# A planned attention + MLP kernel: first loads and clears rearranged, GpSimd casts as plain copies, mixed rows written straight to x, and a rank of its own for every planned operation

## The chip, the cores and the metric

One core of one Trainium2 chip. The metric is device time of one launch in microseconds (us), the median of several runs; less is better. Beside it stands one profiled execution, whose trace is the source of every duration in this text. Engines are PE (TensorE matmul), PEld (TensorE weight load), DVE (VectorE), ACT (ScalarE), POOL (GpSimd) and SP (SyncE, here used only to issue DMAs).

## The reference

Two blocks, one after the other. First a linear attention with exponential features, for batch 8, 8 heads, 576 rows and head size 64:

```python
def phi(x):
    proj = np.einsum('bhsd,df->bhsf', x, w_phi)                      # 64 -> 128 features
    proj = proj - np.max(np.abs(proj), axis=-1, keepdims=True)
    return np.concatenate([np.exp(proj), np.exp(-proj)], axis=-1)    # 256 features
q_p, k_p = phi(q), phi(k)
kv, z = einsum('bhsf,bhsd->bhfd', k_p, v), sum(k_p, axis=2)
attn = einsum('bhsf,bhfd->bhsd', q_p, kv) / (einsum('bhsf,bhf->bhs', q_p, z) + 1e-6)
```

Its heads are laid side by side as x (8, 576, 512). Then a two-layer MLP with layer norm and residual: `xn = (x - mean) / sqrt(var + 1e-6) * g_ln`, `out = x + relu(xn @ w_ch1) @ w_ch2`, with w_ch1 512x2048 and w_ch2 2048x512. Inputs and output are float32; the kernel multiplies in bf16.

## The kernel before

**Tiling.** The batch is cut into four pairs. A pair has 1152 rows, nine tiles of 128: four full tiles of each batch, and a ninth, the *mixed* tile, that holds the last 64 rows of both. Attention runs in 32 *units* of two heads, eight to a pair; units 0 to 3 of a pair belong to its first batch and units 4 to 7 to its second. The MLP of a pair takes its tiles in three groups (4, 3, 2 in the first pair). A group can start when all its rows of x are written, normalized and transposed, so the first group of a pair needs that pair's units 0 to 3, and the mixed tile needs all eight.

**One unit.** q and k are brought to bf16 and transposed: on PE in the first units (L689, mixed rows L697), later by a cast (`cast`, L749-766, on DVE, ACT or POOL) and a DMA transpose on SP (L782). PE makes the projections (L882, L888, L804, L897), DVE takes their absolute maxima (L950, L808), ACT the exponentials (L964, L1058, L967 and the small `em`, `en`), POOL scales v (`vv`, L990-999), PE forms k'v (L1095) and q'kv (L1155, L1163, L1169), and DVE with POOL, or in the first units DVE with ACT, divide and write x. The mixed tile's rows are the special case: the two heads of a unit come out on partition halves 0-63 and 64-127, and one of the two halves lies on the wrong partitions for x. Before, that half goes to a small tile `xs`, and after four units one DMA (`move_rows`, L1120) carries it over; eight such DMAs in all.

**The MLP.** L1420 is the first product (four accumulating matmuls per hidden block), its ReLU runs on ACT or DVE (L1431, L1429), L1489 is the second product, L1454 the last tile's in halves. Results are scaled on ACT or DVE, the residual is added on POOL, and SP stores.

**What sets the order.** The program text does not. Every operation is added to a planner (`Order`) with its possible engines, an assumed duration on each, what it reads and writes, and a rank. `run` plays the program through on these assumed durations: whenever an engine is free, the ready operation of lowest rank goes next, on whichever of its engines is free. The instructions are then emitted in that order, engine by engine, and each engine works its list strictly in order. Where PE has nothing ready in the played-through time and that time is under `WARM = 75.0` us, the planner puts a *filler* on PE's list: a matmul of zeros (L1695). Fillers are ordinary instructions and stay in PE's list whatever the chip does. A rank was before the sum of entries of the table `OFF` (33 stage names, in 13 tables: each of the first eight units has its own, the rest share five) and the operation's latest start worked out backwards:

```python
op.rank = sum(OFF[t][k] for t, k in op.rank) + late
```

DMA issues are planned operations too, each followed by one or more pieces that stand for the transfer. Operations without code (`add("DVE", 3.5, -9.0, None)` and the like, after L1589) stand for the prologue, which is written out by hand at L415-470: loads of w_phi, the identity, clearing of tiles.

Of the kernel before, what the change touches and what calls it, by code (L numbers as in the profile page):

```python
# [11 lines left out]
BF16 = mybir.dt.bfloat16  # L12
# [5 lines left out]
def bcast(ap: bass.AP, dim: int, n: int) -> bass.AP:  # L18
# [20 lines left out]
OFF = (  # L39
    {  # L40
        "load": 291.2, "trans": 545.6, "trans.copy": 61.3, "mixed": 513.4, "mixed.max": -174.1,
        "mixed.exp": 7.7, "mixed.fold": 4.9, "k": 74.4, "k.max": 173.7, "k.em": -451.3,
        "k.exp": 679.6, "en": -537.5, "vv": -95.0, "q": -87.3, "q.max": 488.8, "q.em": 368.3,
        "tails": 57.1, "tails.exp": -236.8, "kv": -216.4, "kv.copy": -163.2, "num0": -302.8,
        "num1": -385.0, "num.dve": 8.3, "g1": 0.0, "g2": 0.0, "g3": 0.0, "put": -147.6,
        "ln": -23.8, "w1": -144.2, "w2": -136.8, "ln.c": -23.8, "ln.t": -23.8,
    },
    {
        "load": 291.2, "trans": 447.4, "trans.copy": 161.0, "mixed": 105.6, "mixed.max": 1.6,
        "mixed.exp": 358.4, "mixed.fold": -27.1, "k": -23.9, "k.max": 92.7, "k.em": -150.0,  # L50
# [12 lines left out]
    },
    {
        "load": 291.2, "trans": 554.4, "trans.copy": 7.7, "mixed": 69.3, "mixed.max": -181.5,
        "mixed.exp": 144.7, "mixed.fold": -51.9, "k": -35.6, "k.max": 154.8, "k.em": 166.9,
        "k.exp": 111.3, "en": -340.2, "vv": -186.8, "q": -229.5, "q.max": 107.7, "q.em": 510.4,
        "tails": 220.4, "tails.exp": -338.9, "kv": -395.7, "kv.copy": 83.0, "num0": -369.5,
        "num1": -379.2, "num.dve": -264.0, "g1": 0.0, "g2": 0.0, "g3": 0.0, "put": 54.2,
        "ln": 107.0, "w1": -144.2, "w2": -136.8, "ln.c": 31.8, "ln.t": 66.5,  # L70
    },
    {
        "load": 272.9, "trans": 530.9, "trans.copy": 207.4, "mixed": 269.7, "mixed.max": -38.1,
        "mixed.exp": 276.4, "mixed.fold": -36.7, "k": 556.5, "k.max": 408.1, "k.em": -190.4,
        "k.exp": 563.2, "en": -354.3, "vv": -281.3, "q": 110.5, "q.max": 541.6, "q.em": 101.1,
        "tails": 326.2, "tails.exp": -391.9, "kv": -247.4, "kv.copy": -205.8, "num0": -198.9,
        "num1": -688.0, "num.dve": -117.6, "g1": -293.1, "g2": -189.2, "g3": -5.0,
        "put": -103.6, "ln": 107.2, "w1": -341.2, "w2": -67.5, "ln.c": 107.2, "ln.t": 107.2,
    },
    {  # L80
        "load": 6.3, "trans": 536.0, "trans.copy": 106.5, "mixed": 212.8, "mixed.max": -321.6,
        "mixed.exp": -375.0, "mixed.fold": 170.2, "k": -2.1, "k.max": 368.9, "k.em": 11.7,
        "k.exp": 156.1, "en": -310.7, "vv": -194.9, "q": 84.5, "q.max": -113.0, "q.em": 400.4,
        "tails": 184.4, "tails.exp": -473.9, "kv": -401.2, "kv.copy": -224.2, "num0": -390.2,
        "num1": -685.7, "num.dve": 7.9, "g1": -233.9, "g2": -41.7, "g3": -19.1, "put": -110.8,
        "ln": -60.0, "w1": -341.2, "w2": -67.5, "ln.c": 107.2, "ln.t": 107.2,
# [273 lines left out]
def kernel(  # L360
# [769 lines left out]
    def a_num(u, part):  # L1130
# [104 lines left out]
        if folded(n):  # L1235
# [19 lines left out]
            if i == 3:  # L1255
                move_rows(u, b, V_put)
# [479 lines left out]
```

## Time and profile before

| | us |
|---|---|
| median of 3 runs (lowest to highest) | 362.01 (361.94 to 362.59) |
| the profiled execution's own time | 362.2 |
| span of its trace | 360.4 |
| PE / DVE / ACT / POOL busy | 354.1 / 250.2 / 264.3 / 208.8 |

The span runs from the first to the last recorded instruction; 1.8 us of the profiled execution lie around it. "Busy" for PE includes the drain of pipelined matmuls and the fillers, so a PE that is busy throughout may still be doing nothing useful. A row of the windows view gives, for a stretch of the span, each engine's busy time with its instruction count in brackets, the granted PE clock as a share of full speed, the mean share of DMA engines busy, and GB/s. A row of the timeline gives start, length, engine, line, operation, output <- input, and in square brackets the engine's idle time before it with what ended it.

### The profile page before, as it was taken

How to read it: one execution, taken by the hardware profiler on the slowest of the kernel's cores; microseconds unless marked ns; L12 is line 12 of the kernel's file. 1: busy time of each engine (PE TensorE's matmuls, PEld its weight loads, DVE VectorE, ACT ScalarE, POOL GpSimd, SP SyncE). 2: the span in 40 equal slices, each digit the busy share in tenths (PEclk: the TensorE clock that was granted, in tenths of full speed). 3: DMA queues.
4: the chain of work that ended last, by engine and by line, in shares of the span. 5: the costliest groups of instructions: out<-in, count | busy, mean ns of one | idle time of the engine just before them, and what ended most of it. 6: DMA issues, size and time to landing. Idle time of an engine off the chain costs nothing.

```text
span 360.4 us, 9697 instructions
## 1 busy us (share of the span) xinstructions
PE 354.1 (98%) x3728; PEld 225.5 (63%) x3728; DVE 250.2 (69%) x575; ACT 264.3 (73%) x580; POOL 208.8 (58%) x363
## 2 busy tenths in 40 slices
PE   7999999999999999999999999999999999999995
PEld 6899966656566655555676555555666665455544
DVE  4788978999889986797779669959896856100001
ACT  1859979689899978796978769858968765364430
POOL 1459795858575658482968478595637484210121
PEclk9999999999999999999999999999999999999999
DMA  7999999999999999998999876976665431600012
GB/s 175 316 232 270 233 235 251 225 269 282 250 184 192 257 232 213 248 185 182 238 292 202 152 194 141 221 190 135 118 88 128 98 88 27 155 31 0 29 60 88
DMA packets 134750, 64.01 MB, mean 178 GB/s; under 512 B 101168, under 2 KB 130224, under 8 KB 134704
## 3 DMA queue, kind: packets, MB, share of 16 engines
q1 hardware_dynamic: 128928, 58.61, 74.2%
q0 software_dynamic: 4256, 4.20, 7.1%
q10 hardware_dynamic: 1520, 0.59, 0.7%
q8 instruction: 29, 0.48, 0.6%
q14 instruction: 17, 0.14, 0.1%
HBM read 36.77 MB, written 9.44 MB: 128 GB/s over the span
## 4 chain that ended last, share of the span: by engine, by line
PE 95%; DMA 2%; DVE 1%; ACTq 0%; ACT 0%; SPq 0%; issue 0%; DVEq 0%
PE b_bank L1420 35%; PE b_bank L1489 34%; PE n_bank L1095 4%; PE a_bank L888 4%; PE n_bank L1695 4%; PE a_bank L1163 2%; DMA qx<-in_k_dram 2%; PE n_bank L1089 1%; PE a_bank L897 1%; PE n_bank L1163 1%; PE a_bank L872 1%; PE b_bank L1454 1%; PE n_bank L1169 1%; PE n_bank L804 1%; PE b_bank L689 1%; PE a_bank L882 1%
## 5 line engine op out<-in xcount | busy, mean ns | idle before, releaser
L1420 PE MATMUL b_bank<-xT,w 128*128 128x384 bf16 (+2 forms) x768 | 146.2, 326 | 0.0
L1489 PE MATMUL b_bank<-w,hT_all 128*128 128x512 bf16 x560 | 142.4, 379 | 0.0
L1420 PEld LDWEIGHTS <-w 128*128 128x128 bf16 x768 | 71.1, 98 | 51.3 <-issue 0.3
L1431 ACT ACTIVATE hT_all<-b_bank 128x384 bf16<-128x384 f32 (+2 forms) x121 | 60.1, 498 | 46.3 <-PE b_bank L1420 45.6
L950 DVE TENSOR_REDUCE m<-a_bank 128x8 f32<-128x1024 f32 x64 | 77.4, 1213 | 18.2 <-PE a_bank L888 13.0
L1489 PEld LDWEIGHTS <-hT_all 128*128 128x128 bf16 x560 | 50.9, 98 | 42.3 <-issue 0.3
L964 ACT ACTIVATE eb<-a_bank 128x1024 bf16<-128x1024 f32 x60 | 61.0, 1040 | 3.8 <-DVE qkT L704 3.0
L1508 POOL TENSOR_TENSOR o<-o,x 128x512 f32<-128x512 f32 x23 | 26.6, 1158 | 49.3 <-ACT o L1502 44.3
L1272 POOL TENSOR_TENSOR x<-numc,rden 128x384 bf16<-128x384 f32 (+1 forms) x56 | 33.9, 612 | 28.3 <-DVE rden L1197 27.5
L990 POOL TENSOR_TENSOR vv<-v,em 128x512 bf16<-128x512 f32 x30 | 31.4, 1047 | 32.6 <-ACT em L955 29.3
L1429 DVE TENSOR_SCALAR hT_all<-b_bank 128x384 bf16<-128x384 f32 (+2 forms) x71 | 39.0, 549 | 7.8 <-PE b_bank L1420 6.5
L967 ACT ACTIVATE qe<-a_bank 128x1024 bf16<-128x1024 f32 x40 | 40.6, 1030 | 3.2 <-PE a_bank L888 1.8
L990 POOL TENSOR_TENSOR vv<-v,en 128x512 bf16<-128x512 f32 x30 | 31.6, 1053 | 0.2
L1341 DVE BATCH_NORM_STATS2 st<-x 128x6 f32<-128x256 bf16 (+1 forms) x68 | 26.5, 427 | 2.4 <-POOL x L1272 2.3
L1497 DVE SCALAR_TENSOR_TENSOR o<-b_bank,rstd,x 128x512 f32<-128x512 f32 x12 | 8.9, 740 | 27.1 <-issue 25.6
L1695 PE MATMUL n_bank<-wz 128*128 128x120 bf16 x381 | 27.6, 223 | 0.0
L1502 ACT ACTIVATE o<-b_bank,rstd 128x512 f32<-128x512 f32 x23 | 15.8, 687 | 14.4 <-PE b_bank L1489 14.2
L1163 PEld LDWEIGHTS <-ea 128*128 128x128 bf16 x448 | 21.5, 97 | 7.2 <-issue 0.2
L1695 PEld LDWEIGHTS <-wz 128*128 128x128 bf16 x403 | 24.4, 102 | 0.8
L1095 PE MATMUL n_bank<-vv,eb 128*128 128x65 bf16 x480 | 24.4, 194 | 0.0
L1095 PEld LDWEIGHTS <-eb 128*128 128x128 bf16 x480 | 20.3, 98 | 4.4
L763 POOL TENSOR_TENSOR b<-qk,one 128x1024 bf16<-128x1024 f32 x11 | 20.8, 1894 | 0.4 <-DMA qkT<-b 0.2
(129 smaller groups left out, 508.8 us busy)
## 6 DMA issues: line engine op xcount, KB each, us to landing
out_dram<-o SPq DMA_DIRECT2D x31, 256.0 KB, 3.1
qk<-in_k_dram SPq DMA_DIRECT2D x12, 512.0 KB, 6.1
qk<-in_q_dram SPq DMA_DIRECT2D x12, 512.0 KB, 7.1
v<-in_v_dram SPq DMA_DIRECT2D x12, 512.0 KB, 5.2
w<-in_moe_w_ch_dram POOLq DMA_DIRECT2D x8, 512.0 KB, 11.5
qk<-in_k_dram SPq DMA_DIRECT2D x8, 256.0 KB, 6.0
v<-in_v_dram SPq DMA_DIRECT2D x8, 256.0 KB, 5.8
qk<-in_q_dram SPq DMA_DIRECT2D x7, 256.0 KB, 6.1
```

The source lines that it names most:

```text
L950: nc.vector.reduce_max(out=m, in_=ps, axis=AX.X, apply_absolute_value=True)
L964: nc.scalar.activation(eb, ps, AF.Exp, scale=(1.0, -1.0)[t])
L967: nc.scalar.activation(qe_bufs[n % 2][:, t].rearrange("p (c h) f -> p h c f", h=2), u["pm", 0].rearrange("p (h c) f -> p h c f", h=2), AF. ...
L990: nc.gpsimd.tensor_tensor(out=u["vv"][:, t, 0:MX, 0:D], in0=vb[:, hh, :].rearrange("p (c d) -> p c d", d=D), in1=bcast(e[:, 0:MX], 2, D), ...
L1095: nc.tensor.matmul(ps[:, t, c // 4, :], EB[:, t, c, :], vv[:, t, c, :], start=False, stop=(t == 0 and c == MX - 1), skip_group_check=True,)
L1163: nc.tensor.matmul(ps[t][:, i, :], ea(u, t, c), KV[:, t, c // 4, :], start=True, stop=True,)
L1272: nc.gpsimd.tensor_tensor(out=x_, in0=num, in1=rd, op=ALU.mult)
L1420: nc.tensor.matmul(st["ps"], w1_sb[:, kc, jj * P : (jj + 1) * P], xT_bufs[(pair * NR + r) % XB][:, kc : m * KC : KC, :], start=(kc == 0), ...
L1429: nc.vector.tensor_relu(h_sb, st["ps"])
L1431: nc.scalar.activation(h_sb, st["ps"], AF.Relu)
L1489: nc.tensor.matmul(ch[t], hT[r, jj][:, rt * P : (rt + 1) * P], w2_sb[:, jj, :], start=(jj == 0), stop=(jj == JC - 1),)
L1695: nc.tensor.matmul(banks[res][i][:, 0:WN] if res else warm, wz, wz[:, 0:WN], start=bool(res), stop=bool(res), skip_group_check=True,)
```

## The change

Four parts.

1. *First loads and clears.* w_phi comes in one DMA of both halves instead of two. The negated identity is made on POOL (a clear and a select) instead of by one DVE multiply; clearing the tails of two `ea` tiles and the second `vx` tile moves from DVE to POOL. The tail loads of v move from ACT's queue to SP's, and the load of ACT's table is added right behind the first main load of q. The assumed prologue durations change accordingly.
2. *POOL casts.* A multiply by a broadcast one becomes `tensor_copy`; the assumed duration of the 1024-column cast goes from 1.87 to 1.02 us, that of the 128-column one from 0.38 to 0.5.
3. *Mixed rows.* Both halves are written straight to x, across partitions where needed; `xs` and the eight DMAs of `move_rows` go.
4. *Ranks.* `OFF` and the backward pass go; a table `RANK` of 2362 integers gives each planned operation its rank by number, in the order in which the operations are added. The numbers came out of a search. The first ones read as follows, with what they belong to: issue of the main loads of unit 0, k 110 (SP) and q 707 (ACT), v 838 (SP); ACT table 753; tail loads of k, halves 0 and 1, 619 and 549 (SP); tail loads of q 1158 and 689 (ACT); tail loads of v 546 and 754 (SP); main loads of unit 1, k 548, q 557, v 825; of unit 2, k 610, q 677, v 1252; of unit 3, k 859, q 779, v 1262 (all SP).

```diff
+RANK = tuple(map(int, """
+515 611 710 638 283 459 110 715 707 715 753 619 716 549 716 1158 717 689 717 838 718 546 719 754
+719 548 720 557 722 379 723 645 825 724 610 729 677 729 1252 729 859 730 779 730 1262 730 852
...
-        latest = {}
-        for op in reversed(self.ops):
...
-                op.rank = sum(OFF[t][k] for t, k in op.rank) + late
+        assert len(self.ops) == len(RANK)
+        for op in self.ops:
+            op.rank = RANK[op.number]
...
-    nc.scalar.dma_start(out=wphi_f[0:D, :], in_=w_phi)
-    nc.scalar.dma_start(out=wphi_f[D : 2 * D, :], in_=w_phi)
+    nc.scalar.dma_start(
+        out=wphi_f,
+        in_=bass.AP(tensor=w_phi.tensor, offset=w_phi.offset, ap=[[0, 2], [F, D], [1, F]]),
+    )
...
+    nident = consts.tile([P, P], BF16, name="nident")
+    nc.gpsimd.memset(nident, 0.0)
+    nc.gpsimd.affine_select(
...
-        nc.vector.memset(eb[:, 2 * MX * P :], 0.0)
+        nc.gpsimd.memset(eb[:, 2 * MX * P :], 0.0)
         ea_bufs.append(eb)
-    clear_vx(vx_bufs[1])
-
-    nident = consts.tile([P, P], BF16, name="nident")
-    nc.vector.tensor_scalar(
-        out=nident, in0=ident, scalar1=minus, scalar2=None, op0=ALU.mult
-    )
+    clear_vx(nc.gpsimd, vx_bufs[1])
...
-                nc.gpsimd.tensor_tensor(
-                    out=out, in0=in_, op=ALU.mult,
-                    in1=bcast(bcast(one[:, 0], 1, in_.shape[1]), 2, in_.shape[2]),
-                )
+                nc.gpsimd.tensor_copy(out=out, in_=in_)
...
-        add(("DVE", "ACT", "POOL"), (Port(0.6), 0.98, 1.87), rank, cast_main, r=[*loaded(u, "q"), *loaded(u, "k")],
+        add(("DVE", "ACT", "POOL"), (Port(0.6), 0.98, 1.02), rank, cast_main, r=[*loaded(u, "q"), *loaded(u, "k")],
...
-            if half == b:
-                dst, w = u["x"][ps_, MX : MX + 1, h * D : (h + 1) * D], [("x", pair, 2, h)]
-            else:
-                i = u["i"] % 4
-                dst, w = xs[ps_, i : i + 1, :], [("xs", b, i)]
-            add("POOL", 0.3, V_put, lambda d=dst, p=ps_: put(d, p, 2, 1), r=rd, w=w)
-        if u["i"] % 4 == 3:
-            move_rows(u, b, V)
+            dst = u["x"][b * 64 : b * 64 + 64, MX : MX + 1, h * D : (h + 1) * D]
+            add("POOL", 0.3, V_put, lambda d=dst, p=ps_: put(d, p, 2, 1), r=rd, w=[("x", pair, 2, h)])
...
-    add("POOL", 1.3, -9.0, None)
+    add("POOL", 4.2, -9.0, None)
     add("SP", 0.72, -9.0, None)
-    add("ACT", 1.85, -9.0, None)
-    add("DVE", 3.5, -9.0, None)
+    add("ACT", 1.3, -9.0, None)
+    add("DVE", 3.88, -9.0, None)
     add("PE", 2.1, -9.0, None)
-    add("DVE", 0.8, -8.9, None, w=["wbk"])
-    add("DVE", 1.1, -8.8, None)
-    add("POOL", 0.7, -8.8, None)
+    add("DVE", 0.47, -8.9, None, w=["wbk"])
     load_main("k", 0, 1, -4.0, "SP")
-    load_tails("k", 0, -3.9, "SP")
     load_main("q", 0, 1, -4.0, "ACT")
-    load_tails("q", 0, -3.9, "ACT")
-    load_main("v", 0, 1, -3.8, "SP")
-    load_tails("v", 0, -3.7, "ACT")
     add(
-        "ACT", 1.3, -1.0,
+        "ACT", 1.3, -3.9,
         lambda: nc.scalar.preload_act_table_set("natural_log_exp_and_others"),
     )
+    load_tails("k", 0, -3.9, "SP")
+    load_tails("q", 0, -3.8, "ACT")
+    load_main("v", 0, 1, -3.7, "SP")
+    load_tails("v", 0, -3.6, "SP")
```

Where a rank was written at the call (`-3.9` and the like), `RANK` now takes its place. The first units' division (`put_row` on DVE or ACT) is changed in the same way as the POOL one shown.

More of the change, by code (lines that the diff above doesn't have):

```diff
@@ L147 @@
+RANK = tuple(map(int, """
[112 rows of a table added]
+""".split()))
 class Op:
@@ L236, in offer @@
             heapq.heappush(events, (op.ready, 1, op.number, op))
-        latest = {}
-        for op in reversed(self.ops):
-            us = [us if isinstance(us, float) else 0.6 for us in op.us]
-            late = min((latest[o.number] for o in op.users), default=1000.0) - op.lag
-            late -= sum(us) / len(us)
-            latest[op.number] = late = late if op.due is None else min(late, op.due)
-            if isinstance(op.rank, tuple):
-                op.rank = sum(OFF[t][k] for t, k in op.rank) + late
+        assert len(self.ops) == len(RANK)
+        for op in self.ops:
+            op.rank = RANK[op.number]
         for op in self.ops:
@@ L423 @@
     make_identity(nc, ident)
+    nident = consts.tile([P, P], BF16, name="nident")
+    nc.gpsimd.memset(nident, 0.0)
+    nc.gpsimd.affine_select(
+        out=nident, in_=nident, compare_op=ALU.not_equal, fill=-1.0, base=0, pattern=[[-1, P]],
+        channel_multiplier=1,
+    )
     wz = consts.tile([P, P], BF16, name="wz")
@@ L467 @@
     w2_loads = {}
-    xs = consts.tile([P, 4, D], BF16, name="xs")
     xc_bufs = [consts.tile([P, n, DM], BF16, name=f"xc{i}") for i, n in enumerate((4, 3))]
@@ L786, in a_trans_dma @@
         rank = rk("trans", n)
-        add(("DVE", "ACT", "POOL"), (0.2, 0.2, 0.38), rank, cast_mixed, r=[*loaded(u, "q"), *loaded(u, "k")],
+        add(("DVE", "ACT", "POOL"), (0.2, 0.2, 0.5), rank, cast_mixed, r=[*loaded(u, "q"), *loaded(u, "k")],
             w=[("b16x", n % NB16)])
-        add(("DVE", "ACT", "POOL"), (Port(0.6), 0.98, 1.87), rank, cast_main, r=[*loaded(u, "q"), *loaded(u, "k")],
+        add(("DVE", "ACT", "POOL"), (Port(0.6), 0.98, 1.02), rank, cast_main, r=[*loaded(u, "q"), *loaded(u, "k")],
             w=[("b16", n % NB16)])
@@ L1113, in a_kv @@
         add(("ACT", "DVE"), (0.28, 0.35), rk("kv.copy", n), copy, r=[("kv", n)], w=[("KV", n % 4)], release=("N", 1), reads="N")
-    def move_rows(u, b, V):
-        half = 1 - b
-        rows = slice(half * 64, half * 64 + 64)
-        def move():
-            nc.sync.dma_start(
-                out=u["x"][b * 64 : b * 64 + 64, MX, :].rearrange(
-                    "p (i two d) -> p i two d", two=2, d=D
-                )[:, :, half, :],
-                in_=xs[rows],
-            )
-        dma("SP", V, 32768, move, row=128, r=[("xs", b, j) for j in range(4)],
-            w=[("x", u["pair"], 2, 2 * j + half) for j in range(4)])
     def a_num(u, part):
@@ L1243, in a_num @@
                 return
[L1244 removed]
+            after = [("x", pair, group_of(pair, t0), h0)]
             for half in range(2):
                 ps_ = slice(half * 64, half * 64 + 64)
[L1247 to L1251 removed]
+                dst = u["x"][b * 64 : b * 64 + 64, MX, (h0 + half) * D : (h0 + half + 1) * D]
                 add(("DVE", "ACT"), (0.19, 0.32), V_put, lambda e, d=dst, p=ps_: put_row(e, d, p),
[L1253 removed]
+                    r=[nk, rn, *after], w=[("x", pair, 2, h0 + half), ("last", n, half)], release=(res, room) if half else None)
                 after = [("last", n, half)]
[L1255 to L1256 removed]
             return
@@ L1557, in moe @@
         return V
-    def stage_table(n):
-        return n if n < H else H + sum(n >= m for m in (H + 4, 2 * H, 2 * H + 4, 3 * H))
     def rk(stage, n):
-        return ((stage_table(n), stage),)
+        return ()
     units, pairs = [], []
```

123 lines of the change are left out of this document (5 added, 118 removed), and 110 rows, old and new, of the table RANK.

## The prediction

> **What bounds the kernel now.** I read the page first (who is busy, when), then the windows view by stage, the fillers alone in that view, PE's waits, and last the timeline of the first 14 us and of the end.
>
> ```profile
> span 360.4 us, 9697 instructions
> ...
> PE 354.1 (98%) x3728; PEld 225.5 (63%) x3728; DVE 250.2 (69%) x575; ACT 264.3 (73%) x580; POOL 208.8 (58%) x363
> ```
>
> PE is the longest engine, but part of that is filler. The filler's line alone (count, shortest/median/longest ns, first and last start), the windows view of that line, and the windows of all engines:
>
> ```profile
> L1695 PEld LDWEIGHTS <-wz x403: 95/98/152, 1.0 to 74.8; 128*128 128x128 bf16 x135
> ```
>
> ```profile
> 0.00:20.00 20.00, 10.64 (x143) 9.59 (x144) 1.00 0.92 255
> 20.00:40.00 20.00, 8.79 (x132) 7.44 (x131) 1.00 1.20 235
> ```
>
> ```profile
> 20.00:75.00 55.00, 55.00 (x844) 41.77 (x842) 49.05 (x114) 46.54 (x100) 41.59 (x75) 1.00 1.16 242
> 75.00:356.00 281.00, 281.00 (x2618) 167.28 (x2617) 188.64 (x424) 208.41 (x466) 159.91 (x272) 1.00 0.76 160
> ```
>
> There are 403 fillers, the last at 74.8 us; 143 lie in the first 20 us and 132 in the next. In the stretch from 20 to 75 us, PE is 55.00 of 55.00 busy only thanks to them. The next three views are PE's waits, the chain that ended last, and PE's groups from 320 to 340 us.
>
> ```profile
> PE n_bank L1692 <- DVE wz L426: 1.0, 1, 1.0
> PE a_bank L882 <- DVE qkT L704: 0.8, 1, 0.8
> PE b_bank L689 <- DMA qk<-in_q_dram: 0.5, 1, 0.5
> PE b_bank L804 <- DVE qkT L704: 0.2, 1, 0.2
> ```
>
> ```profile
> 41.69 1.16 PE b_bank L1695 x22
> ...
> 47.84 1.83 PE b_bank L1420 x8
> ...
> 319.02 7.15 PE b_bank L1420 x44
> ...
> 345.63 7.55 PE b_bank L1489 x35
> 353.19 3.51 PE b_bank L1454 x32
> ```
>
> ```profile
> L1420 PE MATMUL b_bank<-xT,w 128*128 128x384 bf16 x82 | 15.3, 326 | 0.0
> L1489 PE MATMUL b_bank<-w,hT_all 128*128 128x512 bf16 x32 | 8.7, 379 | 0.0
> ```
>
> In the chain a filler costs 1.16/22 = 0.053 us of PE's queue, an L1420 matmul of 384 columns 7.15/44 = 0.163, an L1489 one 7.55/35 = 0.216. Between 320 and 340 us PE therefore did 82 x 0.163 + 32 x 0.216 = 20.3 us of useful work in 20 us: no room there. PE's named waits sum to 2.5 us, all in the first 13 us. So **from 75 us to the last matmul at 353.19 + 3.51 = 356.7 us PE's list runs without a hole, and the time can only be won ahead of 75 us**: the fillers, 403 x 0.053 = 21.4 us, and the 2.5 us of waits. Since PE waits for nobody after 13 us although its list is full of fillers, the list itself sets the pace: the chip is no slower than the planner assumed. A filler less on the list is 0.053 us less, until a real wait appears.
>
> What the fillers stand for is the supply from ACT and DVE. From 20 to 75 us these have 8.5 and 6.0 us idle (55 - 46.54, 55 - 49.05). The start is slow too:
>
> ```profile
> 4.62 0.39 PE L689 MATMUL b_bank<-ident,qk 128*128 128x128 bf16 x4
> ...
> 4.82 0.37 SPq L559 DMA_DIRECT2D qk<-in_q_dram  x1
> 4.83 0.22 DVE L453 CAST wbk<-wphi_f 64x128 bf16<-64x128 f32 x1 [0.46 <-DMA wphi_f<-in_w_phi_dram]
> ...
> 5.21 0.49 DVE L437 MEMSET vx<- 128x520 f32 x1 [0.15 <-issue]
> ...
> 5.96 0.25 DVE L462 TENSOR_SCALAR nident<-ident,minus 128x128 bf16<-128x128 bf16 x1
> 6.13 0.42 DVE L704 COPY qkT<-b_bank 128x512 bf16<-128x512 bf16 x1
> ...
> 6.60 0.61 PE L882 MATMUL a_bank<-wbk,qkT 128*128 128x256 bf16 x4 [0.81 <-DVE qkT L704]
> 7.45 1.31 ACTq L559 DMA_DIRECT2D vx<-in_v_dram  x2
> 7.67 0.37 SPq L559 DMA_DIRECT2D v<-in_v_dram  x1
> ...
> 8.78 0.60 PE L882 MATMUL a_bank<-wbk,qkT 128*128 128x256 bf16 x4
> 8.81 1.02 ACT L964 ACTIVATE eb<-a_bank 128x1024 bf16<-128x1024 f32 x1 [3.00 <-DVE qkT L704]
> ...
> 9.83 0.23 PE L697 MATMUL b_bank<-ident,qx 128*128 128x128 bf16 x1
> ...
> 9.87 2.36 DVE L950 TENSOR_REDUCE m<-a_bank 128x8 f32<-128x1024 f32 x2 [1.31 <-ACT eb L964]
> ...
> 12.14 0.41 DVE L808 TENSOR_REDUCE m<-b_bank 128x2 f32<-128x256 f32 x1
> ```
>
> The reader should see two delays: DVE clears tiles (5.21 to 6.2) while k's transposed tile waits for its copy, and ACT's list holds two v-tail issues (7.45, for 1.31 us) ahead of the first exponential, whose data were ready at about 7.2.
>
> **The change part by part.** The sum is made against the profiled execution, 362.2 us (span 360.4 and 1.8 around it), which is 0.2 above the median of 362.01.
>
> *Start.* The copy at 6.13 loses the clears and the nident multiply ahead of it. k's transposes end at 4.62 + 0.39 = 5.0, so it starts at about 5.05, 1.1 us sooner, and L882 at 5.5. One w_phi transfer instead of two should not be later than the second was (cast at 4.83). The first exponential then starts at about 6.1 instead of 8.81, for its queue holds no v-tail issues: 2.7 us on ACT. But k's maximum must follow that exponential, and q's maximum needs q, whose load set PE's 0.5 us wait at 7.7: copy and products as before put q's L882 at 8.78 to 9.38, and the two maxima end at 9.4 + 1.2 = 10.6 instead of 12.2. The mixed maximum, 12.14 now, follows at about 10.9 if its load still lands by the 9.83 of L697. So the bounds are 0 (that load lands late) and 2.7 (ACT's gain in full); I take the middle one that DVE's chain gives, **1.2 us**. The clears on POOL and the new identity lie in POOL's idle 10.72 us before its first scaling at 13.35:
>
> ```profile
> 13.35 1.05 POOL L990 TENSOR_TENSOR vv<-v,em 128x512 bf16<-128x512 f32 x1 [10.72 <-ACT em L955]
> ```
>
> Uncovered they would cost about what the rows above show on DVE, 0.49 + 0.25 us and the small clears, some 1 us. On SP the two v-tail issues cost some 1.3 us of queue that now lies ahead of later main loads.
>
> *Casts and mixed rows.*
>
> ```profile
> L763 POOL TENSOR_TENSOR b<-qk,one 128x1024 bf16<-128x1024 f32 x11 | 20.8, 1894 | 0.4 <-DMA qkT<-b 0.2
> L995 POOL CAST vv<-em 128x8 bf16<-128x8 f32 x30 | 7.6, 253 | 0.0
> L1205 POOL TENSOR_TENSOR xs<-numc,rden 64x64 bf16<-64x64 f32 x28 | 8.2, 292 | 19.4 <-DVE rden L1197 18.8
> ```
>
> ```profile
> 41.31 4.12 SPq L1120 DMA_DIRECT2D x<-xs  x1
> ...
> 59.38 0.40 POOL L1272 TENSOR_TENSOR x<-numc,rden 128x128 bf16<-128x128 f32 x1 [4.10 <-DVE rden L1197]
> ```
>
> No row shows a long plain copy on POOL. It lies between the 0.25 us of an 8-column cast and the 1.894 us of the two-input form. The two-input form costs (1.894 - 1.05)/512 = 1.65 ns a column between 512 and 1024 columns; half of that for one input, plus 0.2 us of fixed cost, gives 1.04 us. Eleven casts then give back 9.4 us of POOL (0 to 18). After 75 us PE waits for no one, and ahead of it POOL still idles 4.10 us at 59.38: **0** on the path, with -0.3 to +0.3 for what stands behind such a cast. [...] Writing the mixed rows across partitions is shown by no row; nearest is 0.292 us, and twice that would add 28 x 0.29 = 8 us to POOL, spread over its 150 us of idle. The eight removed DMAs held SP once for 4.12 us at 41.31; behind it stood loads for later units. **0**, at best 0.3.
>
> *Ranks.* This is the largest unknown. At worst it wins nothing or loses (below); at best ACT and DVE are packed without idle from 20 to 75 us, which is worth the mean of 8.5 and 6.0, 7.2 us. The first eight units had tables of their own before, so the coarse order of the front was already free; what is new is order within a stage and unit. I take a little over a third, nearer the lower end: **2.6 us**, or 49 fillers.
>
> Sum: 362.2 - 1.2 - 2.6 = 358.4 for a profiled execution, **358.2 us** for the median. Its own range, from the bounds of the two terms taken by halves, is 355.5 to 361.
>
> **The rivals.**
>
> *Much more is won* (356.0 to 352, say 354.0). The first MLP matmul is at 47.84; if the four units that it needs run first and later units wait, ACT and DVE pack and nearly all of 7.2 comes, with 1.2 at the start: 362.0 - 8.4 = 353.6. For it: PE's fillers are still 132 in 20 to 40 us. Against: from 20 to 75 us ACT is already 85% and DVE 89% busy, and the first eight units' ranks could move freely before.
>
> *No change.* PE is full after 75 us, and if the new order has as many fillers and the mixed load lands when it did, the start's gain ends as filler elsewhere: 362.0, within 0.2% (0.72 us), which is what a measurement of this kernel can tell from no change.
>
> *Slower: the tail loads land late.* The rank table issues half of k's tail seventh on SP, behind main loads of units 1 and 2 (ranks 546, 548, 549, 557, 610 come ahead of 619). Now SP's sixth issue is at 4.82 and the seventh at 7.67, since SP waited. Issued at 7.67 and landing after the 6.12 us that the chain's first piece shows,
>
> ```profile
> 1.25 6.12 DMA qx<-in_k_dram
> ```
>
> it is there at 13.8 instead of 9.83, 4.0 us late. From a landing at 9.83 + 1.3 = 11.1 on (the mixed maximum had 1.3 us to spare before 12.14), `em`, the scaling of v and unit 0's tail stand behind it; 13.8 costs 2.7. ACT loses that only where other units' exponentials don't fill in. With nothing won by ranks: 362.0 + 2.7 - 0.5 = 364.2. Such a start would also show as PE waits, since the fillers were counted on the planner's landing. [...]
>
> **How the numbers follow.** Forecast 0.55, much more 0.20, no change 0.10, slower 0.15. Faster by over 0.2% is 0.75, within 0.10, slower 0.15. For the range I leave out the far half of the large-gain case (below 353.5) and most of what is above 363.0: 353.5 to 363.0.
>
> **What would show it.** Right: fillers down from 403 to about 330 to 355; the first L1420 at about 44 instead of 47.84; the first exponential near 6.1; the POOL cast row near 1.04; PE without waits after 75 us and 3.7 us from last matmul to end as now. Wrong: PE waits named by `qx` in the first 15 us (the slow case); fillers unchanged (no change); PE waits or idle after 75 us, which would mean that ranks fitted to assumed durations don't hold on the chip.

## The result and the profile after

| | before | changed |
|---|---|---|
| median of 4 runs each (lowest to highest), us | 362.29 (361.94 to 362.59) | 366.38 (365.43 to 367.07) |
| ratio to before (95% interval) | | 1.0111 (1.0085 to 1.0138) |
| the profiled execution / its span, us | 362.2 / 360.4 | 365.43 / 363.3 |

The change makes the kernel slower by 1.1%, 4.1 us. The forecast was 358.2. Of the 4.1 us the two profiled executions show 3.2 (the changed one's profile was its quickest execution). One execution of e3 (388.69 us, mean PE clock 0.977) and one of e5 (410.25 us, 0.853) below fell in a slower state of the chip and are left out of all medians and ratios.

First the page of the changed kernel (span and busy time), then its filler's own line, then PE's waits (total us, times, longest us). Lines have moved: the filler is L1665 (was L1695), the first MLP product L1395 (L1420), the k and q products L884 (L882), the main transposes L694 (L689).

```profile
span 363.3 us, 9623 instructions
...
PE 354.4 (98%) x3690; PEld 225.3 (62%) x3690; DVE 248.0 (68%) x565; ACT 266.5 (73%) x586; POOL 199.0 (55%) x369
```

```profile
L1665 PEld LDWEIGHTS <-wz x365: 95/98/152, 1.0 to 75.9; 128*128 128x128 bf16 x183
```

```profile
PE b_bank L694 <- DMA qk<-in_q_dram: 1.1, 1, 1.1
PE a_bank L884 <- DVE qkT L709: 1.0, 1, 1.0
PE n_bank L1662 <- DVE wz L437: 1.0, 1, 1.0
PE a_bank L884 <- ACT hT_all L1060: 0.6, 1, 0.6
PE a_bank L899 <- DVE m L952: 0.6, 1, 0.6
PE a_bank L890 <- ACT ea L1060: 0.3, 1, 0.3
PE b_bank L874 <- DVE hl L1010: 0.2, 1, 0.2
PE a_bank L899 <- ACT ea L1060: 0.2, 1, 0.2
```

The first three waits end by 8.0 us, the other five lie between 20 and 69 us, where the kernel before has none.

The useful matmuls are as many as before: 3690 - 365 = 3728 - 403 = 3325. PE's idle time grew from 360.4 - 354.1 = 6.3 to 363.3 - 354.4 = 8.9 us, its busy time by 0.3: together the 2.9 us of span. The busy time grew although 38 fillers, 2.0 us at 0.053 each, are gone. The windows of the early stretch (PE, PEld, DVE, ACT, POOL with counts, granted PE clock, DMA share, GB/s) show why, and the two later windows follow:

```profile
5.00:6.00 1.00, 0.29 (x6) 0.12 (x3) 0.58 (x3) 0.00 (x0) 0.00 (x0) 1.00 1.01 301
6.00:7.00 1.00, 0.61 (x4) 0.31 (x4) 0.28 (x1) 0.01 (x1) 0.00 (x0) 1.00 0.79 177
7.00:8.00 1.00, 0.00 (x0) 0.00 (x0) 0.00 (x0) 1.00 (x1) 0.00 (x0) 1.00 1.15 233
8.00:9.00 1.00, 0.99 (x10) 1.00 (x11) 0.35 (x2) 0.01 (x1) 0.00 (x0) 0.50 0.99 225
9.00:10.00 1.00, 1.00 (x13) 1.00 (x11) 1.00 (x2) 0.00 (x0) 0.00 (x0) 0.50 1.02 300
10.00:11.00 1.00, 1.00 (x9) 0.76 (x7) 0.21 (x1) 0.00 (x0) 0.00 (x0) 0.50 0.71 205
11.00:12.00 1.00, 1.00 (x18) 1.00 (x16) 0.89 (x1) 0.22 (x1) 0.00 (x0) 0.79 1.08 345
```

```profile
20.00:75.00 55.00, 52.87 (x801) 39.86 (x799) 45.23 (x100) 47.21 (x102) 37.37 (x71) 1.00 1.09 234
75.00:356.00 281.00, 281.00 (x2645) 166.64 (x2644) 191.70 (x437) 209.50 (x467) 155.05 (x281) 1.00 0.77 162
```

In 5 to 8 us PE works 0.9 of 3 us, and from 8 to about 11.4 us it is granted half its clock (0.50): 3 x 0.5 + 0.21 = 1.7 us of full speed lost, about what the missing fillers save. After 75 us PE is full, as before. Between 20 and 75 us it is not: it works 52.87 us where the kernel before worked 55.00, so 2.1 of the 2.6 us of new idle time lie there. For a balance, here are the first 20 us of all engines (before, then changed), the fillers alone in 20 to 75 us before, and the fillers alone in both stretches in the changed kernel:

```profile
0.00:20.00 20.00, 17.39 (x265) 16.09 (x266) 12.01 (x38) 9.34 (x15) 7.30 (x18) 1.00 0.92 255
0.00:20.00 20.00, 16.89 (x218) 15.78 (x219) 10.06 (x28) 9.11 (x17) 5.38 (x18) 0.91 0.86 231
```

```profile
20.00:75.00 55.00, 17.76 (x259) 14.78 (x259) 1.00 1.16 242
```

```profile
0.00:20.00 20.00, 10.49 (x133) 9.58 (x133) 0.91 0.86 231
20.00:75.00 55.00, 15.33 (x230) 12.90 (x230) 1.00 1.09 234
```

The first 20 us lose 0.5 us to idle time (3.1 for 2.6) and 1.7 to the clock and save ten fillers, 0.5 us: 1.7 us. The stretch from 20 to 75 us loses 2.1 us to idle time and saves 29 fillers, 1.5 us: 0.6 us. These are estimates at 0.053 us a filler; together they place 2.3 of the 2.9 us of span, most of it in the first 20 us.

Now the head in the timeline of the changed kernel, and two pieces of its chain of waits:

```profile
0.75 1.18 ACTq L418 DMA_DIRECT2D wphi_f<-in_w_phi_dram  x1
...
5.37 0.46 DVE L464 CAST wbk<-wphi_f 64x128 bf16<-64x128 f32 x2 [3.25 <-DMA wphi_f<-in_w_phi_dram]
...
5.86 0.43 DVE L709 COPY qkT<-b_bank 128x512 bf16<-128x512 bf16 x1
...
6.34 0.61 PE L884 MATMUL a_bank<-wbk,qkT 128*128 128x256 bf16 x4 [1.05 <-DVE qkT L709]
...
6.99 1.02 ACT L966 ACTIVATE eb<-a_bank 128x1024 bf16<-128x1024 f32 x1 [2.32 <-PE a_bank L884]
...
7.98 0.61 SPq L564 DMA_DIRECT2D qx<-in_k_dram  x1
...
8.01 0.61 PE L694 MATMUL b_bank<-ident,qk 128*128 128x128 bf16 x4 [1.05 <-DMA qk<-in_q_dram]
...
14.29 0.28 PE L702 MATMUL b_bank<-ident,qx 128*128 128x128 bf16 x2
...
15.58 0.27 PE L806 MATMUL b_bank<-wbk,qkT 128*128 128x256 bf16 x1
...
19.62 1.94 ACT L1060 ACTIVATE ea<-a_bank 128x1024 bf16<-128x1024 f32 x2 [0.70 <-PE a_bank L874]
...
52.12 1.04 POOL L768 CAST b<-qk 128x1024 bf16<-128x1024 f32 x1
```

```profile
50.80 2.59 PE b_bank L1395 x12
...
356.09 3.51 PE b_bank L1429 x32
```

The kernel before has, in its timeline:

```profile
15.14 1.94 ACT L1058 ACTIVATE ea<-a_bank 128x1024 bf16<-128x1024 f32 x2 [0.19 <-PE a_bank L872]
...
28.20 1.96 ACT L1058 ACTIVATE ea<-a_bank 128x1024 bf16<-128x1024 f32 x2
```

The first exponential is earlier (6.99 for 8.81), and so is the first of DVE's maxima (8.99 for 9.87), but the second exponential is later (12.69 for 11.12), and so is unit 0's tail. The first tail exponential (`ea`), with which the head ends here, moves from 15.14 to 19.62: 4.5 us. From there to the first MLP product the new order needs 50.80 - 19.62 = 31.2 us where the old one needed 47.84 - 15.14 = 32.7. It is 1.5 us quicker behind this mark and 4.5 slower up to it; the difference, 3.0, is the growth of the span. The mark does not stand for the same amount of work in both orders, though: the second pair of `ea` exponentials starts at 28.20 before and at 22.48 in the changed kernel. So 4.5 and 1.5 us are sums by this one mark and not prices of two stretches.

```profile
22.48 1.94 ACT ea L1060 x2
...
28.93 1.55 DVE m L952 x2
...
57.78 1.90 ACT ea L1060 x2
```

These are three more pieces of the changed kernel's chain. Between 20 and 75 us it passes through ACT for 9.0 us and through DVE for 10.4; in the kernel before it stays on PE there. By itself that is no price: e7 below shows such a chain without a loss.

### The profile page after: what moved, and what is told of

It reads as the page before. It is cut to its first block, busy times and chain, and to the rows that moved or that the text cites. A ratio compares the mean times of both kernels' runs of the same rounds, so it can differ in the third digit from the quotient of the medians.

```text
span 363.3 us, 9623 instructions
## 1 busy us (share of the span) xinstructions
PE 354.4 (98%) x3690; PEld 225.3 (62%) x3690; DVE 248.0 (68%) x565; ACT 266.5 (73%) x586; POOL 199.0 (55%) x369
## 4 chain that ended last, share of the span: by engine, by line
PE 91%; DVE 3%; ACT 2%; DMA 1%; issue 1%; ACTq 1%; DVEq 0%
PE b_bank L1395 34%; PE b_bank L1464 34%; PE a_bank L890 4%; PE n_bank L1097 4%; PE n_bank L1665 3%; PE a_bank L1150 2%; ACT ea L1060 2%; DMA qk<-in_q_dram 1%; DVE m L952 1%; PE n_bank L1091 1%; PE b_bank L1429 1%; PE n_bank L1150 1%; PE a_bank L899 1%; PE n_bank L1156 1%; PE a_bank L884 1%; PE b_bank L694 1%
## 5 line engine op out<-in xcount | busy, mean ns | idle before, releaser
L1395 PE MATMUL b_bank<-xT,w 128*128 128x384 bf16 (+2 forms) x768 | 145.0, 326 | 0.0
L1464 PE MATMUL b_bank<-w,hT_all 128*128 128x512 bf16 x560 | 144.1, 379 | 0.0
L1395 PEld LDWEIGHTS <-w 128*128 128x128 bf16 x768 | 71.5, 98 | 51.2 <-issue 0.3
L1406 ACT ACTIVATE hT_all<-b_bank 128x384 bf16<-128x384 f32 (+2 forms) x124 | 61.1, 497 | 45.4 <-PE b_bank L1395 44.5
L1464 PEld LDWEIGHTS <-hT_all 128*128 128x128 bf16 x560 | 49.8, 98 | 42.2 <-issue 0.3
L1253 POOL TENSOR_TENSOR x<-numc,rden 128x128 bf16<-128x128 f32 (+1 forms) x56 | 34.6, 623 | 40.5 <-DVE rden L1184 39.3
L1483 POOL TENSOR_TENSOR o<-o,x 128x512 f32<-128x512 f32 x24 | 27.7, 1154 | 53.0 <-ACT o L1477 44.0
L1404 DVE TENSOR_SCALAR hT_all<-b_bank 128x384 bf16<-128x384 f32 (+2 forms) x68 | 36.8, 552 | 11.2 <-PE b_bank L1395 8.7
L1477 ACT ACTIVATE o<-b_bank,rstd 128x512 f32<-128x512 f32 x24 | 16.5, 689 | 18.5 <-PE b_bank L1464 18.1
L1665 PE MATMUL n_bank<-wz 128*128 128x120 bf16 x335 | 24.7, 229 | 0.0
L1192 POOL TENSOR_TENSOR x<-numc,rden 64x64 bf16<-64x64 f32 x56 | 16.7, 298 | 14.5 <-DVE rden L1184 11.3
L1665 PEld LDWEIGHTS <-wz 128*128 128x128 bf16 x365 | 22.7, 104 | 0.1
```

What stands on the lines that cost most here:

```text
L1253: nc.gpsimd.tensor_tensor(out=x_, in0=num, in1=rd, op=ALU.mult)
L1395: nc.tensor.matmul(st["ps"], w1_sb[:, kc, jj * P : (jj + 1) * P], xT_bufs[(pair * NR + r) % XB][:, kc : m * KC : KC, :], start=(kc == 0), ...
L1404: nc.vector.tensor_relu(h_sb, st["ps"])
L1406: nc.scalar.activation(h_sb, st["ps"], AF.Relu)
L1464: nc.tensor.matmul(ch[t], hT[r, jj][:, rt * P : (rt + 1) * P], w2_sb[:, jj, :], start=(jj == 0), stop=(jj == JC - 1),)
L1665: nc.tensor.matmul(banks[res][i][:, 0:WN] if res else warm, wz, wz[:, 0:WN], start=bool(res), stop=bool(res), skip_group_check=True,)
```

## The experiments

"Changed" is the changed kernel, "before" the one before. The two columns of milestones, `ea` (first tail exponential) and MLP (first MLP product), are starts in the timeline of each kernel's one profiled execution, in us; the kernel before has 15.1 and 47.8. The clock is that of the same execution.

| run | median us | ratio to before (95%) | ea | MLP | mean PE clock |
|---|---|---|---|---|---|
| changed | 366.38 | 1.0111 (1.0085-1.0138) | 19.6 | 50.6 | 0.995 |
| e8: before with parts 1 to 3 by hand | 362.54 | 1.0003 (0.9989-1.0018) | 14.7 | 47.3 | 0.998 |
| e3: changed with the old rank rule | 375.95 | 1.0381 (1.0341-1.0420) | 20.5 | 53.8 | 1.000 |
| e1: changed, fillers in the early waits | 366.55 | 1.0095 (1.0057-1.0132) | 18.7 | 50.9 | 1.000 |
| e2: changed, q first on ACT | 365.51 | 1.0073 (1.0046-1.0100) | 18.5 | 49.5 | 0.998 |
| e4: e1 and e2 | 365.75 | 1.0084 (1.0063-1.0104) | 18.7 | 50.3 | 1.000 |
| e5: changed, loads by first use | 366.25 | 1.0104 (1.0069-1.0139) | 19.9 | 51.0 | 0.994 |
| e7: before, half the fillers | 361.89 | 0.9987 (0.9968-1.0006) | 14.6 | 46.6 | 1.000 |
| e6: changed, half the fillers | 364.61 | 1.0066 (1.0041-1.0091) | 18.1 | 49.5 | 1.000 |
| e11: e6 and e2 | 365.23 | 1.0065 (1.0040-1.0090) | 19.1 | 51.3 | 1.000 |
| e9 / e13: changed, 60 / 120 fillers in front | 365.82 / 368.81 | 1.0090 (1.0071-1.0109) / 1.0173 (1.0156-1.0191) | 19.4 / 21.8 | 50.9 / 52.8 | 1.000 / 0.998 |
| e10 / e14: before, 60 / 120 fillers in front | 364.30 / 367.25 | 1.0045 (1.0027-1.0064) / 1.0132 (1.0111-1.0152) | 15.9 / 20.4 | 49.0 / 53.2 | 1.000 / 0.998 |
| e15: changed, w_phi in two transfers | 365.34 | 1.0088 (1.0075-1.0102) | 17.7 | 49.7 | 1.000 |
| e17: e15 and e5 | 365.39 | 1.0068 (1.0043-1.0093) | 17.9 | 50.3 | 0.998 |
| e18: e17 and e1 | 365.19 | 1.0057 (1.0038-1.0077) | 17.5 | 50.6 | 1.000 |
| e12: e7 and e8 | 361.57 | 0.9973 (0.9957-0.9989) | 14.6 | 46.7 | 0.997 |
| e16: e12, w_phi in two transfers | 361.34 | 0.9975 (0.9960-0.9989) | 14.7 | 46.7 | 1.000 |

### Which part: the hand-written ones or the order?

e8 leaves the order of before and puts in the new loads and clears, the copies and the direct rows; e3 leaves these in the changed kernel and takes back the old rule of ranks.

```diff
 # e8, on before (excerpt)
+    nc.gpsimd.memset(nident, 0.0)
...
-                nc.gpsimd.tensor_tensor(
+                nc.gpsimd.tensor_copy(out=out, in_=in_)
```

```diff
 # e3, on changed
-        for op in self.ops:
-            op.rank = RANK[op.number]
+                op.rank = sum(OFF[t][k] for t, k in op.rank) + late
```

> Edit: the kernel before, its plan and order untouched, with the hand-written parts of the change only: one w_phi transfer, the negated identity and the clears on POOL, the first v-tail issues on SP instead of ACT, plain copies for the POOL casts, mixed rows straight to x without the eight DMAs (their places in SP's list are left empty). The prediction's start term says up to 1.2 us faster; if PE's list sets the pace, 0 to 0.5 us. If these parts carry the loss of the changed kernel: 364 or more.

> Edit: the changed kernel with the old table of offsets and its backward pass in place of one rank per operation; loads, clears, casts and mixed rows as changed. Order theory: the first three parts together are worth 0 to 1.5 us of gain, so 360.8 to 362.3, and the first MLP matmul comes before 48 us. If instead the first loads and clears (or casts and rows) are the loss: 364 or more.

e8 brings the first exponential to 7.0 and the first MLP product forward by 0.5 us, and the time stays where it was, 1.0003 (0.9989 to 1.0018). So the 4.1 us come with the new order, or with that order meeting these parts; e15 below takes one of them, the single w_phi transfer, out of the new order. e3 is 14 us slower than before. By its own forecast 364 or more would have meant that parts 1 to 3 are the loss, but e8 has these parts and loses nothing. What e3 loses comes from planning anew with the old tables, so e3 is no clean undoing of part 4 and says nothing of what the new ranks are worth.

### Is it the half clock?

e1 gives PE 18 fillers in each of its two early waits, e2 puts q's main load ahead of its tail load on ACT, e4 does both.

```diff
 # e1, on changed (the same again ahead of main_products for i == 1)
+            if u["n"] == 0 and which == (0,):
+                for _ in range(18):
+                    fill()
 # e2, on changed: operation 8 (q's main load) is issued at the place of 17 (its tail load)
+        at = {op.number: i for i, op in enumerate(done)}
+        done.insert(at[17], done.pop(at[8]))
```

> Edit: the changed kernel with 18 more fillers on PE's list in each of its two early waits (before the first product of unit 0's k, 1.05 us of wait, and before the transposes of its q, 1.05 us). Nothing else moves. Clock theory: in the changed kernel PE's granted clock is 0.50 from about 8.0 to 11.2 us, after these two waits, and the fillers and products behind them take twice their time; with the waits filled the clock stays at 1.00, the first projection of the mixed rows comes at about 14 instead of 15.6, and 1 to 2 us of the 4.1 us loss come back (364.4 to 365.4 against 366.4). Order theory (the new order itself is the loss): clock stays up, but the time changes by less than 0.5 us. Load theory: the same, since the data land when they did.

> Edit: the changed kernel with two DMA issues on ACT's queue swapped, unit 0's main load of q ahead of the first tail load of q. Load theory (the new order brings unit 0's q late, at 7.96 against 7.70, and the planner thought it would be there at 5.7): q lands 0.5 to 0.8 us sooner, PE's wait of 1.05 us shrinks to 0.3 to 0.5, and with the shorter wait the clock may also stay up: 0.5 to 2 us come back. Order theory: below 0.5 us. Clock theory: nothing unless the clock trace changes.

> Edit: the fillers in both waits and the swap of the two q loads together, on the changed kernel. Clock and load theories together: 2 to 3 us come back, 363.4 to 364.4. If the order in 15 to 50 us holds a loss of its own, the first MLP matmul still comes later than the 47.84 of the kernel before.

In e1 the clock is 1.00 throughout, `ea` comes 0.9 us sooner, and the median doesn't change (366.55 for 366.38): no gain from the clock shows. The two intervals leave 0.6 us of gain, +-1.7, so e1 alone doesn't exclude the 1 to 2 us that the clock theory forecast. Executions of one kernel with both clocks don't agree: in e5 the three at 0.994 took 366.21 to 367.41 us and the one at 0.998 took 364.22; in e6 the two at 0.995 took 364.63 and 365.05 us and the two at 0.999 and 1.000 took 364.29 and 364.59; in e15 the one at 0.995 took 365.34, the median. So the clock isn't the whole loss (e1, e4 and e9, with the clock up in every execution, are still 3 us or more above the kernel before); whether it is a part isn't settled. Where e1's 0.9 us went is in its timeline:

```profile
23.09 0.62 PE L697 MATMUL b_bank<-ident,qk 128*128 128x128 bf16 x8 [1.40 <-DMA qk<-in_k_dram]
```

PE reaches a later unit's transposes sooner and waits there for a k load (in e4 0.67 us at 22.53). In the changed kernel the same transposes start at 22.58 without a wait. Of e2's 0.9 us the intervals don't tell whether it is a gain; of the 2 to 3 us forecast for e4, 0.6 came, inside the intervals too.

e5 sorts SP's loads of units 0 to 5 by their planned first use:

```diff
 # e5, on changed (with e2's two lines)
+        for i, op in zip(places, sorted((done[i] for i in places), key=lambda o: need[o.number])):
+            done[i] = op
```

> Edit: the changed kernel with its first loads (all of units 0 to 5) issued on SP in the order in which the planner's own schedule first uses them, in the same places of SP's list, and q's main load first on ACT; every other engine's list as it is. Load theory (the new order issues loads that nothing needs yet, such as unit 5's q seventh on SP, ahead of those that are needed next, and SP runs 2 to 3.3 us behind the plan): PE's first projections come 1.5 to 3 us sooner, the first MLP matmul at 47.5 to 49, and the time falls to 362.5 to 364.5. Order theory: the time stays within 1 us of 366.4, since ACT and DVE are full behind 15 us.

The wait near 22 us is gone, but w_phi lands still later (its cast starts at 6.20 instead of 5.37), `ea` stays at 19.9, and the time stays too. The order of the loads alone isn't it, as far as a version with a later w_phi can tell; e17 below takes it up again.

### Does PE's list set the pace?

e7 (before) and e6 (changed) leave out every second filler behind the first ones; e11 adds e2's edit to e6.

```diff
 # in the emission loop; e7: 14.0, e6: 7.9
+                thin = op.start > 14.0 and not thin
+                if op.start > 14.0 and thin:
+                    continue
```

> Edit: the kernel before without every second filler from 14 us of the plan on (145 fewer, 7.7 us of PE's list); all else as it is. The prediction's step (PE waits for nobody after 13 us, so a filler less is 0.053 us less until a real wait appears): 355 to 359. If the supply is only just in time and the fillers stand where PE would wait anyway: 361 to 363, with waits in their place.

> Edit: the changed kernel without every second filler from 7.9 us of the plan on (154 fillers fewer, 8.2 us of PE's list at 0.053 us each); all else as it is. If PE's list sets the pace of the first 75 us: 5 to 8 us faster than the changed kernel. If the supply (loads, ACT, DVE) sets it: within 1 us of it, with the lost fillers showing as PE waits, and perhaps a lower granted clock.

> Edit: the changed kernel without every second filler from 7.9 us of the plan on, and with q's main load first on ACT. If the two gains seen singly (1.8 us and about 1 us) are of different causes (fillers in the way; a late load): 363.2 to 363.8. If both only keep the clock up and shorten the same wait: 364.5. Order theory: the first MLP matmul stays behind the 47.84 of the kernel before in either case.

In e7 145 matmuls of zeros are gone, 145 x 0.053 = 7.7 us of PE's list. The time moves by 0.13%, with no change inside the interval, far from the 355 to 359 us that the prediction's price of a filler gives. Its page and its waits:

```profile
PE 350.0 (97%) x3583; PEld 219.4 (61%) x3583; DVE 251.3 (70%) x575; ACT 264.1 (73%) x580; POOL 208.3 (58%) x363
```

```profile
PE n_bank L1093 <- DVE KV L1107: 0.8, 1, 0.8
PE b_bank L701 <- DMA qx<-in_q_dram: 0.6, 1, 0.6
```

For the fillers PE now waits: on DVE, on a tail load of q, and in smaller pieces on POOL and ACT. Between 20 and 75 us its chain now passes through ACT for 10.3 us, DVE for 6.6 and POOL for 3.0. The kernel before had no waits after 13 us *because* fillers stood in their place. In the changed kernel half the fillers bring 1.8 us at the median, with intervals that just touch, and the longest of PE's waits names a load:

```profile
PE b_bank L698 <- DMA qk<-in_q_dram: 1.5, 3, 0.7
```

Put together with e2 (e11) the gain doesn't add: 365.23, above each of its forecasts.

### How much of the loss is a head that waits for its data?

e9 and e13 put 60 and 120 more fillers at the very front of the changed kernel's PE list, 3.2 and 6.4 us at 0.053 each; e10 and e14 do so before. If the head's work waits for data anyway, a later start costs nothing.

```diff
-    for _ in range(FIRST):
+    for _ in range(FIRST + 60):
```

> Edit: the changed kernel with 60 more fillers at the very front of PE's list (3.2 us at full clock, some more at the cold start), so that the first loads get a start of some 3 us over everything that computes; all else as it is. To be read against the same edit of the kernel before (e10). Load theory (the new order was planned on loads issued at once, and unit 0's and unit 1's data come 1.9 to 3.3 us later than it planned): most of these 3 us are made up, the first exponential of unit 0's tails comes no later than 1 us behind its 19.6 without the edit, the time is 366 to 367, and the gap to e10 is 1 us or less, of either sign. Order theory (the new order loses whatever the loads do): the time is 368.5 to 370, and the gap to e10 stays at 3 to 4 us.

> Edit: the kernel before with the same 60 fillers at the front of PE's list. Its loads were planned 1.1 us or less too early at the front, so it has less to make up: 364.5 to 365.5, and lateness at the front goes through to the end nearly in full.

> The changed kernel with 120 more fillers at the very front of PE's list (about 6.4 us by 0.053 us each; 60 of them cost it nothing, 365.82 against 366.38). If its loss is that loads land behind the planned order, a second 3.2 us still comes nearly free: 365.5 to 367, first MLP product at 51 to 52. If the order itself sets the pace once the loads are ahead, the second 3.2 us count nearly in full: 368 to 369, first MLP product near 54.

> The kernel before with the same 120 fillers at the front. With 60 it went from 362.29 to 364.30. Both theories expect the second 60 to count in full here: 367 to 367.5, first MLP product near 52. Late loads as the whole of the loss: the gap to the changed kernel with 120 closes to within 0.5 us or turns round (its order is 1.7 us quicker behind the head). A loss in the order itself: the gap stays at 1.5 us.

The first 60 cost the changed kernel nothing (365.82 for 366.38) and the kernel before 2.0 us, 0.2 less than the lowest that was forecast for it. The gap goes from 4.1 to 1.5 us (0.45%, by the two intervals +-0.27). The second 60 cost both about 3.0 us, and the gap stays at 1.6. So **about 2.6 us of the 4.1 lie in a head in which the changed kernel's PE started too early for its data, and about 1.5 us do not** (each gap is known to about 1 us, the 2.6 to about 1.4). The half clock that followed those early waits is in the 2.6: e9's executions have clocks of 0.999 to 1.000. The timeline of e9 shows that its first transposes may come 3.8 us later (8.10 for 4.28) and `ea` and the first MLP product still come when they did:

```profile
19.44 1.94 ACT L1060 ACTIVATE ea<-a_bank 128x1024 bf16<-128x1024 f32 x2 [0.70 <-PE a_bank L874]
...
23.04 0.62 PE L694 MATMUL b_bank<-ident,qk 128*128 128x128 bf16 x8 [0.62 <-DMA qk<-in_k_dram]
...
50.89 2.75 PE L1395 MATMUL b_bank<-xT,w 128*128 128x512 bf16 x12
```

Where the remaining 1.5 us lie is not settled. In e9 against e10 the first MLP product is 1.9 us later; in e13 against e14 it is 0.4 sooner, and e13's profile has 1.6 us of waits for `KV` and a DMA transpose between 150 and 250 us. These are single executions, 0.7 (e13) and 1.4 us (e14) above their medians. One place to look is PE's waits for DVE and ACT near 37, 60 and 68 us, 0.59, 0.20 and 0.34 us: they stand unchanged in the profiles of the changed kernel, e2, e4, e5, e9, e13 and e15, however the head went, and the kernel before has none there. That they cost time isn't shown; in e7 new waits of this size cost nothing that could be told.

### Can the head be mended?

e15 loads w_phi in two transfers again. e17 joins that with e5, e18 adds e1's fillers.

```diff
-    nc.scalar.dma_start(
-        out=wphi_f,
-        in_=bass.AP(tensor=w_phi.tensor, offset=w_phi.offset, ap=[[0, 2], [F, D], [1, F]]),
-    )
+    nc.scalar.dma_start(out=wphi_f[0:D, :], in_=w_phi)
+    nc.scalar.dma_start(out=wphi_f[D : 2 * D, :], in_=w_phi)
```

> The changed kernel with w_phi loaded in two transfers again (64 partitions each), as before. If the single transfer, whose cast starts at 5.37 against 4.83, holds back the first product (6.34) and so part of the head: w_phi cast near 4.8, first product near 5.9, and 0.3 to 0.5 us less, 365.9 to 366.1. If the head's end is set by PE's list and by later loads: first product sooner, mixed rows still at 15.6, and no change in the time.

> The changed kernel with w_phi in two transfers (alone 365.34) and SP's loads of units 0 to 5 in the order in which they are first used, q first on ACT (alone 366.29). If late loads make the part of the loss that a later start absorbs: first tail exponential by 17.7, no wait of PE on a k load near 22 us, first MLP product at 48.5 to 49.5, time 364 to 365. If the loads are not it: first MLP product stays at 49.7 or later and the time at 365.3 or above.

> As e17, with 18 fillers in each of PE's two early waits. With the k load near 22 us out of the way, loads theory: no later than e17, 364 to 365, clock 1.00 throughout. If the changed order sets the rest: 364.0 is a floor, 1.5 us above the kernel before. If the fillers only lengthen PE's list: 0.5 to 1.9 us more than e17.

Two lines of e15's timeline, one of e18's:

```profile
4.96 0.22 DVE L462 CAST wbk<-wphi_f 64x128 bf16<-64x128 f32 x1 [0.98 <-DMA wphi_f<-in_w_phi_dram]
...
21.97 0.62 PE L692 MATMUL b_bank<-ident,qk 128*128 128x128 bf16 x8 [0.78 <-DMA qk<-in_k_dram]
```

```profile
39.09 0.40 PE L711 MATMUL b_bank<-ident,qk 128*128 128x128 bf16 x4 [1.97 <-DMA qk<-in_q_dram]
```

In e15 the last cast ends at 5.18 instead of 5.83, the clock stays at 1.00, and `ea` comes 1.9 us sooner; the median is 1.0 us less, but the two intervals overlap. PE waits near 22 us again. In e18 that wait is gone, and one of 1.97 us for a q load stands at 39 us: on SP the next q load behind the tail loads, the first of which holds SP for 3.79 us at 30.25 (SP's longest wait there, 3.8 us, names PE), goes out at 36.10 (34.15 in the changed kernel). So the first MLP product stays at 50.6. Both runs miss the 364 to 365 of the loads theory by a few tenths. By its first MLP product (50.3) and its time e17 lies on the side of its forecast on which the loads are not it; but in it, too, a new wait of 1.24 us for a q load has come, at 38.78, so the loads are not excluded. e18 is quicker than the changed kernel by 0.54%, +-0.33, and still slower than before.

### A version that beats both

e12 keeps the order of before, with half the fillers (e7) and parts 1 to 3 (e8); e16 is e12 with w_phi in two transfers.

> Edit: the kernel before, order untouched, with the hand-written parts of the change and without every second filler from 14 us of the plan on. Singly these gave a first MLP matmul at 47.3 and 46.7 (47.84 before) and no change of time that could be told. If supply ahead of 75 us sets the time: 361.0 to 361.8. If ACT and DVE give back every early microsecond later: 362.3, as before.

> The order of before with the hand-written parts and without every second filler (361.57), w_phi in two transfers again. If the single transfer delays the head: 361.1 to 361.4. If not: 361.5 to 361.8.

Both are faster than the kernel before by 0.25% to 0.27%, and their intervals exclude no change: 361.57 and 361.34 us. Neither half showed a gain alone. e12's time is in the range forecast for it if supply ahead of 75 us sets the time. e16's is in the range forecast if the single transfer delays the head, but its interval is e12's, so that cost doesn't show here. e16's page:

```profile
span 359.3 us, 9395 instructions
...
PE 349.0 (97%) x3583; PEld 218.9 (61%) x3583; DVE 247.6 (69%) x569; ACT 264.2 (74%) x580; POOL 200.5 (56%) x370
```

## Why the prediction was wrong

**The step that failed first is the reading of the fillers**: "Since PE waits for nobody after 13 us although its list is full of fillers, the list itself sets the pace ... A filler less on the list is 0.053 us less, until a real wait appears." The supply of data from ACT, DVE, POOL and the loads set the pace, and its waits were hidden under the fillers. e7 shows it on the kernel before: 7.7 us less of list, 0.5 us less of time, an interval that holds zero, and a chain that leaves PE for ACT, DVE and POOL as soon as fillers go. Neither the 21.4 us of fillers nor a count of 49 of them was a price. The changed kernel has 38 fillers less and loses 4.1 us.

**Ranks: 2.6 us won.** The term has the wrong sign; the order costs about 4 us. Its upper bound, 7.2 us of ACT's and DVE's idle time in 20 to 75 us, was not approached: by the window above ACT now idles 55 - 47.21 = 7.8 us there and DVE 9.8, on the mean 8.8, so the new order packs these engines no tighter. The bound also looked only at 20 to 75 us, and by e9 and e10 most of the loss is ahead of it. The prediction named the mixed rows' place only by when their load lands. In the new order they stand behind the next unit's transposes and products: a k tail load goes out at 7.98, the median from issue to landing is 5.0 us for such loads, so it is there at about 13 (an estimate), and its transposes start at 14.29 without a wait, behind 35 fillers and other units' products.

**Start: 1.2 us won.** Parts 1 to 3 alone (e8) are worth 0.0, with 0.4 us at the most inside the interval. "One w_phi transfer instead of two should not be later than the second was" failed: it takes 1.18 us to issue, its cast starts at 5.37 instead of 4.83, the copy of k's transposes at 5.86 instead of the 5.05 of the prediction, the first exponential at 6.99 instead of 6.1. The gain in the first exponential was real, and worth nothing, as the prediction allowed with its lower bound.

**Casts and mixed rows: 0.** Right: the copy takes 1.04 us, as estimated from the two-input rows (that one input costs half of two was an assumption, for before shows no long plain copy on POOL), and POOL's gain moves nothing (e8). The 56 writes of mixed rows on POOL take 0.298 us each, where 28 of them took 0.309 and the 28 for `xs` 0.292: writing them across partitions costs nothing extra.

**The rivals.** "Slower: the tail loads land late" had the right sign and forecast the late issue of that load (7.67; it was 7.98, though ninth on SP and not seventh), at 364.2 for the 366.38 that came. What it put behind the load did come late: `em` at 17.87 (13.05 before), the first scaling of v at 18.22 (13.35) and the tail. But no wait of PE names `qx`; the order itself puts this work late, and PE's waits in the head are for w_phi's cast and copy and for q. "Much more is won" and "no change" are excluded by the interval.

**The signs.** Fillers 365 (330 to 355 foretold), first MLP product 50.6 (44), no waits of PE after 75 us and 363.3 - 359.6 = 3.7 us behind the last matmul (both as foretold). None of the signs listed under "wrong" appeared, and the forecast was wrong: two of the three sought a wait on PE, in the first 15 us or behind 75, while new waits came between (2.1 us) and PE's list hides others; the third, unchanged fillers, took a filler for a price.

## What to carry to other kernels

Where an engine that works its list in order is fed with fillers (the changed kernel's PE stands idle for 1.05 us ahead of 8.01 with 324 fillers still on its list), neither its busy share nor its lack of waits says that it sets the pace: before, PE was 98% busy and waited for nobody after 13 us, and 7.7 us less of list moved the time by 0.13% (e7). So take out half of the fillers and see whether the time moves. A new order is to be judged first by its head: what arrives when, against when its first consumer asks; putting more work in front of the engine in both kernels (e9, e10) shows cheaply how much of a loss is waiting for data. In these runs a start that was mended at one load moved the wait to the next one (e1, e15, e18).

## What the runs showed of the hardware

- **Half clock after a short lull.** From the end of the fillers at about 5.3 us to 8.0 us PE worked 0.61 us, in two waits of 1.05 us each by the trace, and was then granted 0.50 for 3.4 us. With less of a gap (e15's profile, where the same product starts at 5.70 and PE is busy for 2.1 of the 3 us from 5 to 8, for 0.9 in the changed kernel) or with fillers in it (e1), 1.00 was kept. In e15 one execution of five still had a mean clock of 0.995. So what came before the fall was 2.7 us, and not idle throughout. What the half clock cost in time isn't settled (e1, e5, e6).
- **One DMA of 128 partitions against two of 64.** The single w_phi transfer took 1.18 us to issue and its data were cast at 5.37; the two took 0.57 and 0.62 us in e15 and were cast at 3.74 and 4.96.
- **Loads at the head take 4 to 5 us to land.** With a DMA share of about 1 in most of the head's windows, the median from issue to landing of the q, k and v loads in the first 18 us of the changed kernel was 4.3 to 5.3 us, by kind of load.
